# The sequence stage of a gated spectral/ReGLU kernel written as one bilinear form of 26 block products

## The chip, the core and the metric

The kernel runs on one core of a Trainium2 chip. The metric is the device time of one execution in microseconds, a median of runs. All data are float32 in HBM; a product of two float32 matrices is made of three fp32r matmuls (below).

## The reference

x has 2048 rows (positions) of 512 features, F is 1792. What is computed:

```
g = sigmoid((x * gate_w).sum(-1))
a = x @ dft_hid_re.T ; b = x @ dft_hid_im.T          # feature transform, 2048 x 512
y = dft_seq_re @ a - dft_seq_im @ b                  # sequence transform, 2048 x 2048 each
B = (relu(x @ W_gate) * (x @ W_up)) @ W_down         # ReGLU
out = g * y + (1 - g) * B
```

The change concerns the second line of the transforms, y. In the kernel dft_seq_re is called cr and dft_seq_im ci; both lie in HBM in tiles of 128 x 2 x 512 (512 KB).

## The kernel before

**One queue per engine.** Nothing loops on the chip. Python code records operations with a key, the number of matmuls after which the operation is thought to stand (op, pe), and class Plan then orders them: `due` gives each a latest time, `order` simulates the engines with fixed costs and picks what goes next on each, `run` emits the instructions in that order (all from one line, so every instruction of the profile has the line L126). On the chip each engine carries out its own queue in order; only semaphores between engines and DMAs hold it up. A key holds nothing up: a DMA that depends on nothing is issued as soon as its queue comes to it. Loads go through SP's queue (`load`), stores and accumulating DMAs (destination += source) through POOL's (`store`, `accumulate`). There are 8 semaphores for the DMAs of each of the two queues, so that a ninth waits for the first of eight.

**Split products.** A float32 operand is split in hi = its fp32r rounding (ACT, one CAST) and lo = raw - hi (DVE, one TENSOR_TENSOR); a product takes PARTS = (lo,hi), (hi,lo), (hi,hi), three matmuls. Names ending in h and l are those halves (ch, cl the two halves of a tile of Cr or Ci, wah and wal those of weights).

**SBUF** is cut into 51 units of 4 KB a partition, which the planner hands out (`buf`). PSUM is 8 banks, used as four pairs x, m, y, t (`Pair`).

**The stages, in PE's order.** A warm-up of 18 bf16 matmuls; then the two start blocks of the gate and up products (`Block`, seven products in place of eight for each 2 x 2 grid of blocks, order ORDER_S), whose tiles x11, x21, x12, x22 of x and wr of the weights are the first 12 DMAs on SP (x22 is the twelfth; DVE adds it into xs, the right side of the sixth of seven products, and wb0l is the lo part of a sum of weights of the first block, which stands behind that xs in DVE's queue); the further gate and up blocks (`Joined`, `JointX`, `JointW`), h stored to hd; the gates g (`gate`, gd); the feature transform (`Spectral`, `SpectralBlock`), whose result goes to ad in HBM; the down product (`Down(0)`, `Down(1)`, which put z, already multiplied by 1 - g, into out); then the sequence stage.

**The sequence stage before** is the last 1296 matmuls, some 291 us. It is a set of Strassen-like products with the right sides from Cr or Ci and the left sides from ad: `Joint((0,))` and `Joint((1,))` (the rows with x = 3, one for Cr and one for Ci), `Opening` twice for Cr, `Shorter` twice for Ci, and `Joint((0, 1), last=True)`. Their right sides are raw tiles or sums of tiles. `Round` and `Sequence` load raw tiles (r) and form the sums on DVE, the last of each with an accumulating DMA straight into SBUF; the Joints read theirs from td in HBM, where `joint_sums` (a copy from HBM to HBM, then an accumulation onto it) and `own_sums` (on DVE, from loaded tiles) have put them, with keys from 180 on. A product's result is taken out of PSUM at its turn, multiplied by the gate (gg) and accumulated into out. `Joint.evac` has the last rows of the kernel: the last product is made in two halves of 256 columns, each multiplied by the gate, added to what out held (jv) and stored.

Of the kernel before, what the change touches and what calls it, by code (L numbers as in the profile page):

```python
# [9 lines left out]
F32R = mybir.dt.float32r  # L10
# [19 lines left out]
FIRST = (1, 5)  # L30

# [247 lines left out]
def kernel(ctx: ExitStack, tc, xP, xG, wgu, wd, cr, ci, wri, gw, out):  # L279
# [73 lines left out]
    def combine(o, a, b, sign):  # L353
        (plan.vector.tensor_add if sign > 0 else plan.vector.tensor_sub)(o, a, b)
# [367 lines left out]
    class SpectralBlock:  # L722
# [47 lines left out]
        def out(self, f, key):  # L770
            (a11, a21), (a12, a22) = ([self.o[f"{f + 1}{j}"][:, k] for k in range(2)] for j in (1, 2))

            def keep(n, t, k=2):
                o = ad[f, n:n + k, self.q, :, 2 * self.ih:2 * self.ih + 2].rearrange("x p t n -> p x t n")
                store(o, t if k == 2 else t.unsqueeze(1))

            op(key, keep, 0, a11, 1)
            op(key, keep, 1, self.o[f"{f + 1}2"].all)
            if f == 0:
                return op(key, keep, 3, a21, 1)  # L780
            u, v = (buf(f"as{n}", (2, 2, HD)) for n in range(2))
            op(key, lambda: combine(u[:, 0], a21, a22, -1))
            op(key, lambda: combine(u[:, 1], a21, a11, -1))
            op(key + 4, lambda: combine(v[:, 0], a11, u[:, 0], -1))
            op(key + 4, lambda: combine(v[:, 1], a12, v[:, 0], -1))
            op(key + 6, keep, 3, u.all)
            op(key + 10, keep, 5, v.all)
# [35 lines left out]

    class Spectrum:


        FORM = {1: 0, 2: 1, 4: 2, 5: 3, 7: 4, 6: 5, 3: 6}

        def __init__(self):
            self.t = {}  # L830

        def get(self, m, n, key, step=8):
            raw = buf(f"l{m}", [4, HD])
            hi, lo = self.t[m, n] = [buf(f"l{x}{m}", [4, HD], F32R) for x in "hl"]
            op(key - 60, lambda: load(raw.all, ad[1, self.FORM[m], n]))
            op(key, lambda: E().scalar.copy(hi.all, raw.all))
            op(key + step, lambda: E().vector.tensor_sub(lo.all, raw.all, f32(hi.all)))

        def late(self, key):
            for m, k in ((1, 0), (5, 48), (6, 60), (7, 120), (4, 192)):  # L840
                for n in range(2):
                    self.get(m, n, key + k - 88 + 12 * n)

    SUM = {5: 40, 6: 40, 7: 44}
# [106 lines left out]
    class Sequence(Round):  # L951
        HI, LO, ONE, keep = 31, 24, 1, staticmethod(accumulate)
        FRESH = ()

        def __init__(self, left, m, p):
            self.m, self.p = m, p
            self.g = gate_row(0, (2 * p, 2 * p + 1), plan.now + 10)
            super().__init__(left, (2, 2, 2, 2))

        def parts(self):  # L960
            return [(x, jj) for x, js in ((1, 4), (5, 4), (6, 4), (3, 2), (7, 4), (3, 4), (4, 4))
                    for jj in (range(js) if (x, js) != (3, 4) else (2, 3))]

        def source(self, b, jj):
            return (cr, ci)[self.m][2 * self.p + int(b[1]) - 1, int(b[0]) - 1, jj]

        def rights(self):
            for jj in range(4):
                r = {b: buf(f"r{b}") for b in BLOCKS if b != "21"}
                for b, key in self.loads(jj):  # L970
                    op(key - 90, lambda r=r, b=b, jj=jj: load(r[b].all, self.source(b, jj)))
                for x, o, i, key in self.sums(jj):
                    if x == 4:
                        op(key, lambda r=r, o=o, jj=jj: accumulate(r[o].all, self.source("21", jj)))
                    else:
                        op(key, lambda r=r, o=o, i=i: combine(r[o].all, r[o].all, r[i].all, 1))
                for x, b in self.TILES:
                    self.split(x, jj, r[b])

        TILES = (1, "11"), (5, "11"), (6, "11"), (3, "22"), (7, "12"), (4, "11")  # L980

        def loads(self, jj):
            at = self.at
            return ("11", at[1, jj]), ("12", at[5, jj]), ("22", at[6, jj] - 10)

        def sums(self, jj):
            at = self.at
            return ((5, "11", "12", at[5, jj] - 40), (7, "12", "22", at[7, jj] - 44), (6, "11", "22", at[6, jj] - 40),
                    (4, "11", "21", at[6, jj] + 4))

    class Opening(Sequence):


        FRESH = (7, 1)
        TILES = (7, "22"), (1, "11"), (6, "22"), (5, "12"), (4, "22")

        def parts(self):
            return [(x, jj) for x, js in ((1, (0, 1)), (7, range(4)), (1, (2,)), (6, range(4)), (1, (3,)), (5, range(4)), (4, range(4)))
                    for jj in js]

        def loads(self, jj):
# [8 lines left out]
        def evac(self, x, key):  # L1010
# [9 lines left out]
            elif x == 4:  # L1020
                self.end(key)
# [421 lines left out]
```

## Time and profile before

| | |
|---|---|
| median of 3 runs | 779.41 us (779.22 to 779.71) |
| profiled execution, span | 777.9 us |
| matmuls | 3414, of them 18 for the warm-up |
| DVE, ACT, POOL instructions | 736, 499, 178 |
| HBM read, written | 155.45 MB, 74.73 MB |
| granted TensorE clock | full speed in all 40 slices |

The page gives the busy time of each engine and its share of the span; the chain is the work that ended last, followed back from the last instruction. A row of the timeline has start, length, engine, line, operation, out<-in, count, and in brackets the idle time of that engine before it and what ended it. The row of a stretch (windows) has, after its two ends and its length, the busy time of PE, PEld, DVE, ACT and POOL, then the granted clock, the DMA engines' mean busy share and GB/s. Rows of DMA issues end with the size and the time from issue to landing. q1 is SP's queue, q0 POOL's.

### The profile page before, as it was taken

To read this page: it belongs to the slowest core of one execution; us is meant where nothing else is said; L and a number is where in the kernel's file an instruction comes from. 1 tells how busy PE (TensorE), PEld (TensorE's weight loads), DVE (VectorE), ACT (ScalarE), POOL (GpSimd) and SP (SyncE) were. 2 spreads that over 40 slices of the span, in tenths; PEclk is the share of its full clock that TensorE was granted. 3 is DMA by queue.
4 is the path that set the end of the run, shared out by engine and by line. 5 is a ranking of instruction groups with operands and counts; after the bars stand their busy time and mean duration, and the time that the engine had idled before them with its cause. 6 is when DMAs were issued, how large, how long until landed. Compare 5 with 4: busy or idle time off the path is not lost.

```text
span 777.9 us, 9558 instructions
## 1 busy us (share of the span) xinstructions
PE 772.3 (99%) x3414; PEld 638.3 (82%) x3414; DVE 665.5 (86%) x736; ACT 425.9 (55%) x499; POOL 121.5 (16%) x178
## 2 busy tenths in 40 slices
PE   9999999999999999999999999999999999999997
PEld 7888888888888888888888888888888888888886
DVE  6999766766778685999996999998699899699898
ACT  6666444434455443566653667547644755345791
POOL 0021333332222332211000000030002011001000
PEclk9999999999999999999999999999999999999999
DMA  9246497999897999775369789989989997999982
GB/s 324 82 150 163 162 267 227 314 300 251 229 322 281 337 408 405 276 279 187 94 208 380 267 262 389 373 172 266 310 294 206 356 306 167 284 250 305 388 278 55
DMA packets 60255, 205.65 MB, mean 264 GB/s; under 512 B 7152, under 2 KB 7664, under 8 KB 60208
## 3 DMA queue, kind: packets, MB, share of 16 engines
q1 hardware_dynamic: 37264, 122.72, 43.5%
q0 software_dynamic: 22944, 82.32, 39.2%
q8 instruction: 27, 0.44, 0.2%
q14 instruction: 20, 0.16, 0.1%
HBM read 155.45 MB, written 74.73 MB: 296 GB/s over the span
## 4 chain that ended last, share of the span: by engine, by line
PE 98%; DMA 1%; SPq 0%; ACT 0%; DVE 0%; issue 0%; DVEq 0%
PE ps L126 98%; DMA x<-xP 1%; SPq L126 0%; DVE jo L126 0%; ACT xh L126 0%; ACT wah L126 0%; DVEq L126 0%
## 5 line engine op out<-in xcount | busy, mean ns | idle before, releaser
L126 PE MATMUL ps<-ch,ll 128*128 128x512 f32 x516 | 200.7, 389 | 0.0
L126 PE MATMUL ps<-cl,lh 128*128 128x512 f32 x516 | 200.7, 389 | 0.0
L126 PE MATMUL ps<-ch,lh 128*128 128x512 f32 x516 | 200.7, 389 | 0.0
L126 ACT CAST ch<-r 128x1024 fp32r<-128x1024 f32 x80 | 82.1, 1054 | 74.1 <-DVE r L126 64.6
L126 PEld LDWEIGHTS ps<-ch,ll 128*128 128x128 f32 x516 | 96.9, 188 | 20.1
L126 PEld LDWEIGHTS ps<-cl,lh 128*128 128x128 f32 x516 | 96.9, 188 | 20.1
L126 PEld LDWEIGHTS ps<-ch,lh 128*128 128x128 f32 x516 | 96.9, 188 | 20.0
L126 DVE TENSOR_TENSOR cl<-r,ch 128x1024 fp32r<-128x1024 f32 x80 | 95.6, 1221 | 7.7 <-ACT ch L126 6.1
L126 ACT CAST ch<-hr 128x1024 fp32r<-128x1024 f32 (+1 forms) x56 | 51.8, 945 | 43.5 <-DVE hr L126 21.2
L126 DVE TENSOR_TENSOR jcl<-jc,jch 128x1024 fp32r<-128x1024 f32 x56 | 65.6, 1222 | 7.8 <-issue 3.9
L126 ACT COPY s<-ps 128x1024 f32<-128x1024 f32 (+1 forms) x52 | 46.0, 884 | 47.6 <-PE ps L126 46.3
L126 ACT CAST jch<-jc 128x1024 fp32r<-128x1024 f32 x56 | 56.2, 1052 | 16.1 <-PE ps L126 14.0
L126 DVE TENSOR_TENSOR cl<-hr,ch 128x1024 fp32r<-128x1024 f32 (+1 forms) x56 | 60.1, 1087 | 5.1 <-ACT lh L126 2.7
L126 ACT ACTIVATE ps<-ps 128x512 f32<-128x512 f32 (+1 forms) x42 | 33.0, 785 | 55.0 <-PE ps L126 52.6
L126 POOL DMA_DIRECT2D out<-z x20 | 14.6, 729 | 297.3 <-DVE z L126 290.0
L126 DVE TENSOR_TENSOR r<-r,r 128x1024 f32<-128x1024 f32 x48 | 57.6, 1220 | 0.2
L126 DVE TENSOR_TENSOR u<-ps,s 128x1024 f32<-128x1024 f32 x28 | 34.1, 1221 | 13.4 <-PE ps L126 8.8
L126 POOL DMA_DIRECT2D hd<-h x35 | 23.0, 662 | 136.9 <-DVE h L126 125.6
L126 PE MATMUL ps<-xh,wb0l 128*128 128x512 f32 x112 | 43.8, 391 | 0.0
L126 PE MATMUL ps<-xh,wb0h 128*128 128x512 f32 x112 | 43.6, 389 | 0.0
L126 PE MATMUL ps<-xl,wb0h 128*128 128x512 f32 x112 | 43.6, 389 | 0.0
L126 PE MATMUL ps<-xh,wb1l 128*128 128x512 f32 x112 | 43.6, 389 | 0.0
(161 smaller groups left out, 1536.1 us busy)
## 6 DMA issues: line engine op xcount, KB each, us to landing
hr<-hd SPq DMA_DIRECT2D x33, 512.0 KB, 5.1
jc<-td SPq DMA_DIRECT2D x32, 512.0 KB, 8.1
td<-ci POOLq DMA_DIRECT2D x24, 512.0 KB, 10.1
r<-cr SPq DMA_DIRECT2D x24, 512.0 KB, 9.5
r<-ci SPq DMA_DIRECT2D x24, 512.0 KB, 8.5
out<-z POOLq DMA_DIRECT2D x20, 512.0 KB, 7.2
l<-ad SPq DMA_DIRECT2D x18, 512.0 KB, 8.7
wr<-wgu SPq DMA_DIRECT2D x16, 512.0 KB, 8.3
```

The costliest lines, as they stand in the source:

```text
L126: getattr(getattr(nc, self.engine), self.name)(*map(ap, self.a), **{k: ap(x) for k, x in self.k.items()})
```

## The change

y is now written as one bilinear form. Cr and Ci are taken together as a 4 x 4 grid of blocks (`block`), the feature transform as a 4 x 2 grid, and 26 products of a sum of the first with a sum of the second are added, with signs, to the 4 x 2 grid of y. TURN is the order of the products, SIDE names for each product the sum that is its right side (r), its left side (l) and the place that it is added to (o), SUMS how each sum is made of two others (sign last). Each product has four parts of 12 matmuls of 512 columns (two row tiles i, two k, three PARTS): cr and ci, two halves each.

`form_stored` puts nine of these sums, four parts each, into td by a copy from HBM to HBM and an accumulation onto it (three values from key 80 on, five from 400, one before Down(0)), `form_rights` two more by loads, DVE and a store, `form_lefts` four left sums into ad. The other sums are made in the stage: on DVE (`combine`) or, for the values in DRAWN and LDRAWN, by an accumulating DMA into the tile that is held in SBUF. `walk` decides what is held, loaded and dropped with 6 tiles (r) and 4 (l) for a part; LEAD says by how many matmuls ahead of the product's key each is done (in front of hi and lo). `Joins` holds the sums of results in PSUM pairs or, as js, in SBUF; where the next product needs the pair at once, the copy or addition is cut in two halves (`each`). The old Sequence, Opening, Shorter, Joint, Spectrum, joint_sums, own_sums and the left sides la and lb are gone, and the feature transform no longer forms sums (as) on DVE.

```diff
--- before.py
+++ after.py
+TURN = (14, 7, 10, 20, 21, 23, 13, 5, 2, 19, 6, 17, 24, 25, 11, 16, 22, 8, 4, 3, 1, 0, 18, 15, 9, 12)
+SUMS = {
+    "r": ((2, 6, -1), (6, 10, 1), (13, 15, -1), (12, 13, 1), (0, 1, 1), (9, 11, -1), (8, 17, 1), (3, 16, -1),
...
+SIDE = {
+    "r": ((26, -1), (7, 1), (29, 1), (31, -1), (32, -1), (33, 1), (22, 1), (34, -1), (25, -1), (35, 1), (16, -1),
...
+FORMED = (16, 17, 18, 19, 20, 21, 28, 30, 36, 37, 38)
+DRAWN = {34: 21, 40: 19, 42: 17, 33: 15, 29: 28, 43: 20, 25: 20, 31: 30, 26: 21}
+FLIP_T, FLIP_K = (1, -1, -1, 1), (1, 1, 1, -1)
+LFORMED = (8, 9, 11, 15)
+LDRAWN = {21: 11, 25: 8}
+ROOM = {'r': 6, 'l': 4}
+LEAD = {'r': {'load': 40, 'sum': 48, 'sums': 6, 'draws': 40, 'hi': 40, 'lo': 32}, 'l': {'load': 40, 'sum': 70, 'sums': 8, 'draws': 40, 'hi': 45, 'lo': 38}}
+RAMP = 60
...
-    ad = hbm("ad", 2, 7, 2, P, 4, HD)
+    ad = hbm("ad", 2, 8 + len(SUMS["l"]), P, 4, HD)
-    td = hbm("td", 2, 2, 4, 2, P, 2, N)
+    td = hbm("td", len(FORMED), 2, 2, P, 2, N)
...
-        (plan.vector.tensor_add if sign > 0 else plan.vector.tensor_sub)(o, a, b)
+        if sign:
+            (plan.vector.tensor_add if sign > 0 else plan.vector.tensor_sub)(o, a, b)
+        else:
+            plan.vector.scalar_tensor_tensor(o, a, -1.0, b, op0=OP.mult, op1=OP.subtract)
...
         def out(self, f, key):
...
+            for j in range(2):
+                n = 2 * (2 * self.q + j)
+                o = ad[f, n:n + 2, :, 2 * self.ih:2 * self.ih + 2].rearrange("x p t n -> p x t n")
+                op(key, lambda o=o, j=j: store(o, self.o[f"{f + 1}{j + 1}"].all))
...
+    def form_rights(values, first, last):
+        formed("r", 16, trails("r", 16, values), range(4), first, last, right_of, "rt", (2, N))
+    def form_stored(values, first, gap):
+        for n, (v, part) in enumerate((v, part) for v in values for part in range(4)):
+            a, b, _ = SUMS["r"][v - 16]
+            for i, (f, x) in enumerate(((store, a), (accumulate, b))):
+                op(first + gap * (2 * n + i), lambda f=f, x=x, v=v, part=part: f(right_of(part, v), right_of(part, x), max_dma_last_dim=8 * N))
+    def form_lefts(values, first, last):
+        formed("l", 8, trails("l", 8, values), (0, 2), first, last, left_of, "lt", (4, HD))
...
+    class Sequence:
...
+        def at(self, turn, part=0):
+            return self.base + 48 * turn + 12 * part
+        def ready(self, turn, part):
+            key = self.at(turn, part)
+            return key - max(0, RAMP - (key - self.base) / 2)
...
+            when, turn = [0] * len(plans), None
+            for n in reversed(range(len(plans))):
+                if plans[n][0] != turn:
+                    turn, key = plans[n][0], lead["sum"]
+                kind = plans[n][1]
+                if kind in ("sum", "draw"):
+                    key += lead[kind + "s"]
+                when[n] = key + lead["load"] if kind == "load" else key
...
+                    if kind == "load":
+                        b = held[v] = buf(side, shape)
+                        op(at, lambda b=b, v=v, part=part: load(b.all, source(part, v)))
+                        last[id(b)] = at
...
+                    elif kind == "draw":
+                        o = held[v] = held.pop(how[0])
+                        at = max(at, last.get(id(o), -999) + 1)
+                        op(at, lambda o=o, y=how[1], part=part: accumulate(o.all, source(part, y)))
+                        last[id(o)] = at
...
+            joins = Joins(self)
+            for turn, product in enumerate(TURN):
+                (rv, rg), (lv, lg), (ov, og) = (SIDE[x][product] for x in "rlo")
+                ps, fresh, sign = joins.begin(turn, ov, SIGNS["r"][rv] * rg * SIGNS["l"][lv] * lg * og)
+                for part in range(4):
+                    c = self.split("c", (2, N), *r[turn, part], False)
+                    if part % 2 == 0:
+                        w = self.split("w", (4, HD), *l[turn, part], sign < 0)
+                    pe(12, self.product, ps, w, c, part, fresh)
+                joins.end(turn, ov)
+        def product(self, ps, w, c, part, fresh):
+            hh = part % 2
+            for i in range(2):
+                for k in range(2):
                     for n, (a, b) in enumerate(PARTS):
-                        mm(ps, l[a][:, 2 * hh + i], c[b][:, i, cols], start=x in FIRST and begin and i == n == 0,
-                           stop=x not in (1, 5, 6, 7) and end and i == 1 and n == 2)
+                        mm(ps[i], w[a][:, 2 * hh + k, i * P:(i + 1) * P], c[b][:, k],
+                           start=fresh and part == k == n == 0, stop=part == 3 and k == 1 and n == 2)
...
+        def each(self, split, f, *a):
+            key = self.at(self.turn + 1) - 1
+            if not split:
+                self.early = 0
+                return op(key, lambda: f(*(x.all for x in a)))
+            for n in range(2):
+                op(key - self.early * (1 - n), lambda n=n: f(*(x[n] if isinstance(x, Pair) else x[:, n] for x in a)))
...
+        def tail(self, x, sign, t, d, g, key):
+            o, v = buf("z"), buf("v")
+            op(key - 100, lambda: load(v.all, od[t, :, 2 * d:2 * d + 2]))
+            for i in range(2):
+                op(key, lambda i=i: E().vector.scalar_tensor_tensor(o[:, i], x[i], float(sign), g.all, op0=OP.mult, op1=OP.mult))
+                op(key, lambda i=i: combine(o[:, i], o[:, i], v[:, i], 1))
+                op(key, lambda i=i: load(od[t, :, 2 * d + i], o[:, i]))
...
-    for n in range(4):
-        joint_sums(n // 2, 2, n % 2, 180 + 110 * n)
-    for n in range(2):
-        own_sums(0, 3, n, 1200 + 100 * n)
-    for n in range(2):
-        joint_sums(1, 3, n, 620 + 110 * n)
+    form_stored([16, 18, 19], 80, 11)
+    form_stored([20, 21, 28, 30, 36], 400, 18)
+    form_rights([17, 37], 1100, 1500)
...
-    la = Left(lambda b, n: ad[0, {"11": 0, "12": 1, "22": 2, "21": 3}[b], n])
-    lb = Spectrum()
...
+    form_stored([38], plan.now - 20, 20)
     Down(lw, 0)
...
+    form_lefts([8, 9, 11, 15], plan.now - 250, plan.now + 50)
     Down(lw, 1)
-    Joint((0,), "xm", 3, [la.side(3, n) for n in range(2)])
-    opened = Opening(la, 0, 0).carry()
-    lb.late(plan.now + 324)
-    Joint((1,), "xm", 3)
-    Opening(la, 0, 1)
-    Shorter(lb, 1, 1)
-    opened.resume(plan.now - 10)
-    Shorter(lb, 1, 0)
-    Joint((0, 1), "xm", last=True, lead=(80, 30))
+    Sequence().run()
```

**What moves.** POOL's queue from its first DMA on, names with their buffer numbers and what a row waits for (DVE is DVE's semaphore, DMASW0 to 7 those of POOL's own DMAs); hd<-h are the stores of the first blocks' h, td sums of Cr or Ci tiles. Before:

```order
L126 DMA hd_68<-h0_214 128x512 [waits DVE_49] x2
L126 DMA hd_68<-h0_242 128x512
L126 DMA hd_68<-h0_242 128x512 [waits DVE_49]
L126 DMA hd_68<-h1_428 128x2x512 [waits DVE_49]
L126 DMA hd_68<-h1_449 128x2x512 [waits DVE_49]
L126 DMA td_70<-cr 128x1024
L126 DMA td_70<-cr 128x1024 [waits DMASW6_49]
```

After:

```order
L262 DMA td_70<-cr 128x1024 x2
L262 DMA td_70<-cr 128x1024 [waits DMASW0_49]
L262 DMA td_70<-ci 128x1024
L262 DMA td_70<-cr 128x1024 [waits DMASW1_49]
L262 DMA td_70<-ci 128x1024
L262 DMA td_70<-ci 128x1024 [waits DMASW3_49]
L262 DMA td_70<-cr 128x1024
L262 DMA td_70<-ci 128x1024 [waits DMASW5_49]
L262 DMA hd_68<-h0_214 128x512 [waits DVE_49]
L262 DMA hd_68<-h0_214 128x512 [waits DMASW2_49,DVE_49]
```

Nine transfers into td, the first two without a wait, now stand ahead of the first store of h; before they began behind six of these stores.

DVE's last rows; cl, jcl are lo parts, wl that of the left side, ps is PSUM, gg the gate, jv and v what out held. Before:

```order
L126 TENSOR_TENSOR jcl_6208<-jc_5982,jch_6180 128x1024
L126 TENSOR_TENSOR jo1_6192<-ps_75,js_6052 128x512
L126 TENSOR_TENSOR jo1_6192<-jo1_6192,gg_5990 128x512
L126 TENSOR_TENSOR jo1_6192<-jo1_6192,jv1_6012 128x512
L126 TENSOR_TENSOR jo0_6231<-ps_75,gg_5990 128x512
L126 TENSOR_TENSOR jo0_6231<-jo0_6231,jv0_5870 128x512
L126 TENSOR_TENSOR jo0_6231<-ps_75,gg_5990 128x256
L126 TENSOR_TENSOR jo0_6231<-jo0_6231,jv0_5870 128x256
L126 TENSOR_TENSOR jo0_6231<-ps_75,gg_5990 128x256
L126 TENSOR_TENSOR jo0_6231<-jo0_6231,jv0_5870 128x256
```

After:

```order
L262 TENSOR_TENSOR wl_6006<-l_5776,wh_5997 128x1024
L262 TENSOR_TENSOR cl_6013<-r_5897,ch_5932 128x1024
L262 TENSOR_TENSOR cl_6020<-r_5919,ch_5948 128x1024
L262 TENSOR_TENSOR z_6027<-ps_75,gg_5869 128x1024
L262 SCALAR_TENSOR_TENSOR z_6048<-ps_75,gg_5953 128x512
L262 TENSOR_TENSOR z_6048<-z_6048,v_5923 128x512
L262 SCALAR_TENSOR_TENSOR z_6048<-ps_75,gg_5953 128x512
L262 TENSOR_TENSOR z_6048<-z_6048,v_5923 128x512
```

The last product is no longer cut into halves of 256 columns: its four rows have 512 each, and ahead of them stands the multiplication of the product before it.

POOL's queue in the first third of the sequence stage (r, r22 and l are tiles in SBUF that the DMA adds to; z and jo go to out). Before:

```order
L126 DMA out<-z21_3937 128x1024 [waits DMASW4_49,DVE_49]
L126 DMA out<-jo1_4047 128x1024 [waits DMASW5_49,DMASW1_49,DVE_49]
L126 DMA out<-jo0_4054 128x1024 [waits DMASW6_49,DVE_49]
L126 DMA out<-z12_4188 128x1024 [waits DMASW7_49,DMASW6_49,DVE_49]
L126 DMA r22_3953<-cr 128x1024 [waits DMAHW3_49,DMASW0_49,Activation_49]
L126 DMA r22_3980<-cr 128x1024 [waits DMAHW0_49,Activation_49]
L126 DMA r22_4005<-cr 128x1024 [waits DMAHW2_49,DMAHW6_49,DMASW2_49,DVE_49]
L126 DMA r22_4033<-cr 128x1024 [waits DMAHW0_49,DMAHW5_49,DMASW3_49,DVE_49]
L126 DMA out<-z21_4490 128x1024 [waits DMASW4_49,DVE_49]
```

After:

```order
L262 DMA r_3613<-td_70 128x1024 [waits DMAHW2_49,DMAHW4_49,DMASW5_49,DVE_49]
L262 DMA r_3654<-td_70 128x1024 [waits DMASW6_49,DVE_49]
L262 DMA r_3690<-td_70 128x1024 [waits DMAHW2_49,DMASW7_49,DVE_49]
L262 DMA r_3723<-td_70 128x1024 [waits DMASW0_49,DVE_49]
L262 DMA r_3912<-td_70 128x1024 [waits DMASW1_49,DVE_49,PE_49]
L262 DMA r_3936<-td_70 128x1024 [waits DMASW2_49,DMAHW3_49,DVE_49,PE_49]
L262 DMA l_3599<-ad_69 128x1024 [waits DMAHW4_49,DMASW3_49,Activation_49]
L262 DMA r_3958<-td_70 128x1024 [waits DMASW4_49,DVE_49]
L262 DMA r_3983<-td_70 128x1024 [waits DMASW5_49,DVE_49,PE_49]
L262 DMA l_3698<-ad_69 128x1024 [waits DMASW6_49,Activation_49]
```

Accumulations into r come in groups of four with the stores of z between, now from td, and into l from ad; before there was one such group for each round.

More of the change, by code (lines that the diff above doesn't have):

```diff
@@ new lines, in trails @@
+def trails(side, blocks, values):
+    left, found = {v: SUMS[side][v - blocks][:2] for v in values}, []
+    while left:
+        ends = [x for e in left.values() for x in e]
+        x = min(ends, key=lambda x: (1 - ends.count(x) % 2, x))
+        trail = [(x, None)]
+        while True:
+            v = next((v for v, e in left.items() if x in e), None)
+            if v is None:
+                break
+            a, b = left.pop(v)
+            x = b if x == a else a
+            trail.append((x, v))
+        found.append(trail)
+    return found
```

512 lines of the change are left out of this document (252 added, 260 removed), and 7 rows, old and new, of the table SUMS.

## The prediction

> **What bounds the kernel now.** I read the page first, then the chain, then what ended PE's waits.
>
> The page's busy times, DMA queues and chain, and three pieces of the chain in order of time (start, length, what):
>
> ```profile
> PE 772.3 (99%) x3414; PEld 638.3 (82%) x3414; DVE 665.5 (86%) x736; ACT 425.9 (55%) x499; POOL 121.5 (16%) x178
> q1 hardware_dynamic: 37264, 122.72, 43.5%
> q0 software_dynamic: 22944, 82.32, 39.2%
> PE 98%; DMA 1%; SPq 0%; ACT 0%; DVE 0%; issue 0%; DVEq 0%
> 11.23 761.70 PE ps L126 x3366
> 774.28 0.42 DVE jo L126
> ```
>
> PE runs without a gap from 11.23 us to 772.93 us. So the time is start + matmuls + tail. One matmul of 512 columns costs 761.70 / 3366 = 0.2263 us (the few of 256 columns pull this down a little; between two starts in the middle of the trace lie 0.227 us). DVE is 86% busy and the 16 DMA engines 43.5 + 39.2 = 83%: neither sets the time, but neither is far from it, and whatever holds PE up once is paid in full, because nothing later on PE is idle that could take it in.
>
> The span of the profiled execution is 777.9 us, the median of the timed runs 779.41 us: 1.5 us lie around the span, and I add them at the end.
>
> **Matmuls taken out.** Counted in the sequence stage: before 1296 matmuls, 24 of them of 256 columns; after 26 products x 4 parts x 12 = 1248, all of 512. Outside the stage nothing changes on PE. That is 36 of 512 and 24 of 256 columns fewer, worth 36 + 12 = 48 of 512: 48 x 0.2265 = **-10.9 us**. This holds where PE stays fed.
>
> **DVE and ACT in the stage.** DVE has 671 rows for 712, and its load falls. The tightest row of before:
>
> ```profile
> 480.00:520.00 40.00, 40.00 (x178) 33.13 (x177) 39.74 (x38) 24.40 (x27) 4.87 (x6) 1.00 0.91 304
> L126 DVE TENSOR_TENSOR cl<-r,ch 128x1024 fp32r<-128x1024 f32 x80 | 95.6, 1221 | 7.7 <-ACT ch L126 6.1
> ```
>
> At 480 to 520 us DVE was busy 39.74 of 40 us and PE still did not wait. After, one turn is 48 matmuls = 10.9 us, and the 1.13 us between starts of such rows (1221 ns, pipelined) lets 9.6 of them pass. The densest place is the end of turn 23: four js rows, one cl, three multiplications by the gate and then the lo part of the next weights, 9 x 1.13 = 10.2 us. That fits by 0.7 us. Some turns begin on a PSUM pair that ACT or DVE has just copied or added in two halves; six matmuls (1.36 us) cover a half of 0.6 to 0.7 us. I count these at **0**; the cover gone would cost 0.5 us each, for six places at most 3 us.
>
> **The tail.** Last rows of before on DVE, and the stores behind them:
>
> ```profile
> 773.03 0.42 DVE L126 TENSOR_TENSOR jo<-ps,gg 128x256 f32<-128x256 f32 x1 [0.38 <-PE ps L126]
> 771.96 0.69 DVE L126 TENSOR_TENSOR jo<-jo,jv 128x512 f32<-128x512 f32 x1
> out<-jo SPq DMA_DIRECT2D x2, 256.0 KB, 3.1
> out<-jo SPq DMA_DIRECT2D x2, 128.0 KB, 1.9
> ```
>
> Before, from PE's end to the last DVE row's end 1.8 us pass (772.93 to 774.70), then a store of 128 KB (1.9 us to landing). After, two of the four last rows, of 512 columns each, remain behind the last matmuls, 0.69 + 0.69 = 1.4 us, and a store of 256 KB, 3.1 us. So -0.4 + 1.2 = **+0.8 us**, between 0 (if the store lands as the small one) and 1.5.
>
> **The POOL queue at the start.** This is the term that decides. POOL carries out its queue in order and waits only for semaphores. Rows of POOL, SP, ACT, DVE and PE in before (start, length; in brackets the idle time before and what ended it):
>
> ```profile
> 17.84 0.71 POOL L126 DMA_DIRECT2D hd<-h  x1 [17.39 <-DVE h L126]
> 51.71 0.56 POOL L126 DMA_DIRECT2D td<-cr  x1
> 4.71 0.88 PE L126 MATMUL ps<-xh,wah 128*128 128x512 f32 x2
> 6.41 0.74 SPq L126 DMA_DIRECT2D x<-xP  x1
> 15.99 1.05 ACT L126 CAST xh<-x 128x1024 fp32r<-128x1024 f32 x1 [0.53 <-DMA x<-xP]
> 17.44 1.22 DVE L126 TENSOR_TENSOR xs<-x,xs 128x1024 f32<-128x1024 f32 x1
> 18.57 0.69 DVE L126 TENSOR_TENSOR wb0l<-ws,wb0h 128x512 fp32r<-128x512 f32 x1
> 19.57 0.40 PE L126 MATMUL ps<-xh,wb0l 128*128 128x512 f32 x1
> 10.00:22.00 12.00, 11.46 (x51) 9.11 (x50) 11.75 (x16) 9.38 (x14) 0.71 (x1) 1.00 1.03 411
> 22.00:50.00 28.00, 28.00 (x124) 22.79 (x123) 27.86 (x36) 18.50 (x24) 2.35 (x4) 1.00 0.18 67
> ```
>
> Before, the first DMA on POOL waits for DVE's h until 17.84 us, and the first sum of Cr blocks (td) goes out at 51.71 us. In the DMA-heavy start (share 1.03 from 10 to 22 us) SP's queue is therefore alone. After, nine td transfers, 5 copies and 4 accumulations, stand ahead of the first hd<-h, and the first two wait for nothing: they go out at about 0.7 us. The planner's key of 80 matmuls stands in no semaphore. They share the engines with the loads that PE waits for.
>
> The software queue's share from 2 to 22 us, and from issue to landing of POOL's first transfer and of the first td row, each alone in its window:
>
> ```profile
> q0 software_dynamic: 16, 0.07, 0.8%
> hd<-h POOLq DMA_DIRECT2D x1, 256.0 KB, 6.0
> td<-cr POOLq DMA_DIRECT2D x1, 512.0 KB, 5.7
> ```
>
> Price of one, from a window in which both queues were loaded (600 to 609 us; packets, MB, share), POOL's packets there being accumulations almost alone:
>
> ```profile
> q0 software_dynamic: 337, 1.22, 68.4%
> q1 hardware_dynamic: 334, 1.23, 36.4%
> ```
>
> A packet of the hardware queue took 0.364 x 9 x 16 / 334 = 0.157 us of one engine, an accumulating one 0.684 x 9 x 16 / 337 = 0.292 us. At 82.32 MB / 22944 packets, 512 KB are 146 packets: 1.43 us of all 16 engines for a copy, 2.66 us for an accumulation. All nine: 5 x 1.43 + 4 x 2.66 = 17.8 us. And the queues took turns packet by packet (337 to 334), so SP's loads do not go first.
>
> [...]
>
> What the loads can stand: x22, issued at 6.41 us, landed at 15.99 us. DVE needs it for xs at 17.44 us, and behind xs stands wb0l, 1.13 + 0.69 us, which PE takes at 19.57 us. So xs may start at 17.75, and x22 land 1.8 us late, at no cost; what is beyond that, D, stops PE, and DVE with it. x22 is the last load of the first two blocks that is close to its use.
>
> - Lower end: only the first two copies get in ahead, on the first loads, which have no such slack (PE waits for them at 4.71 us): D = 2 x 1.43 = 2.9 us.
> - Upper end: all nine before x22: 17.8 - 1.8 = 16.0 us.
> - Between: the accumulations wait for the copy they add to. A td transfer took 5.7 us to land in a quiet stretch, more in a full one, so the chain copy, accumulation, copy passes POOL's six first rows (4 copies, 2 accumulations = 11.0 us) by about 12 us, and the last three rows (6.8 us) start at 17 to 22 us, when x22 would be still outstanding. Six wholly and a quarter of the other three: 11.0 + 1.7 - 1.8 = **+10.9 us**. I take this.
>
> From 22 to 50 us the DMA share was 0.18, so the loads behind x22 find room for the rest.
>
> **DMA in the sequence stage.** After, accumulations rise from 57 to 83 and POOL's share of the engines with them; SP's loads fall from 142 to 116 of 512 KB in the stage.
>
> ```profile
> 520.00:580.00 60.00, 60.00 (x267) 49.69 (x266) 51.78 (x50) 36.99 (x40) 2.54 (x3) 1.00 0.94 294
> 580.00:640.00 60.00, 60.00 (x266) 49.73 (x265) 57.25 (x51) 34.42 (x36) 8.62 (x10) 1.00 0.98 281
> r<-cr POOLq DMA_DIRECT2D x4, 512.0 KB, 14.9
> ```
>
> The engines were already 94 to 98% busy there. By the prices above, an estimate for the whole span: SP's queue 338 us less 26 x 1.43, POOL's 305 us plus 26 x 2.66 and some copies, 680 us together of 768, 89%. An accumulation into r took 14.9 us to land (560 to 600 us). The code puts it 88 matmuls (19.9 us) ahead of PE's use and 48 (10.9 us) ahead of its hi part. So the slowest of before would be 4 us late for its hi part, with 5 us left for hi and lo (1.05 + 1.22 us): not late for PE. I count **0**; lower end 0, since PE has no wait there to lose; upper end 8 us, if each of the eleven groups of accumulations (nine into r, two into l) held PE up by 0.7 us.
>
> **Sum.** 777.9 - 10.9 + 0.8 + 10.9 + 0 = 778.7 us of span, + 1.5 = **780.2 us**: the matmuls saved are given back at the start.
>
> **Rivals.**
> - *The start is cheap.* D is 2.9 to 6 us: the copies from HBM to HBM get few turns while SP's queue is full. For it: hd<-h, issued at 17.84 us into a full queue, is a store of 256 KB that took 6.0 us to land. Against it: two td rows need nothing and are ahead of the first load. Time: 777.9 - 10.9 + 0.8 + 2.9 to 6 + 1.5 = 772.2 to 775.3 us. [...]
> - *Accumulations land late* (the other side). The start costs what I say, and in the sequence stage accumulations into r and l land too late. ACT stands at the hi part, PSUM copies and the next hi parts queue behind it, then lo on DVE, and PE waits for those. By the lead of 19.9 us less hi, lo and a row or two ahead of each in their queues, it decides from a landing of about 15.5 us on. Price 3 to 8 us: 783.2 to 788.2 us. For it: DMA at 89%, 14.9 us already seen. Against it: PE waited nowhere in such stretches before.
> - *The matmuls do not vanish as counted*, or the start costs nothing at all: D = 0 gives 769.3 us. The rows of POOL are against this.
>
> **Chances.** Forecast 0.50, cheap start 0.28, late accumulations 0.20, nothing lost 0.02. A measurement of this kernel tells apart about 0.2%, 1.56 us: faster is below 777.85 us, slower above 780.97. Within the forecast D spreads from 6 to 16 us: below 8.6 is faster (0.08), to 11.7 the same (0.24), above slower (0.18). With the rivals: faster 0.38, same 0.24, slower 0.38. The forecast's own range, D from 8.5 to 14, is 777.8 to 783.3 us. The whole range must take in the cheap start and most of the late accumulations: 771.5 to 787.
>
> **What would show it.** POOL's timeline: td rows from about 0.7 us on, the first hd<-h later than 17.84 us. The DMA queues between 2 and 22 us: a software share of 30 to 60% where before it had 0.8% (right), or under 15% (cheap start). PE's waits: a sum of some 11 us ended by xh, xl or wb0l rows, all before 35 us, x22 landing at about 28 us. Behind that PE should run on to its end with no wait over 0.5 us; waits ended by ACT ch or DVE cl between 470 and 760 us show late accumulations. From PE's end to the span's end: 5.8 us for 5.0. Wrong altogether would be a PE that waits for DVE at the starts of turns, or a gap at turn 24.

## The result, and the profile after

The changed kernel took 788.45 us (median of 4 runs, 785.71 to 790.74), the kernel before 779.47 us beside it (779.22 to 779.71): ratio 1.0114, 95% interval 1.0092 to 1.0135. It is slower, and it lies above the range of 771.5 to 787 us. Its runs also lie 5 us apart, those of the kernel before 0.5 us. The profiled execution took 788.1 us, with a span of 786.3 us.

The page of the changed kernel, busy times, DMA queues and chain:

```profile
PE 769.3 (98%) x3354; PEld 631.9 (80%) x3354; DVE 643.1 (82%) x694; ACT 402.8 (51%) x472; POOL 147.7 (19%) x212
q0 software_dynamic: 28608, 103.56, 50.4%
q1 hardware_dynamic: 32800, 109.08, 37.4%
PE 73%; DMA 13%; issue 6%; DVE 4%; POOL 2%; ACT 1%; SPq 0%; POOLq 0%; DVEq 0%; ACTq 0%
```

The 60 records of matmuls fewer, the lighter DVE and ACT and POOL's larger share are as counted. But PE is only 73% of the chain: DMAs and DVE have come into it. What ended PE's waits:

```profile
PE ps L262 <- ACT wah L262: 3.8, 2, 3.6
PE ps L262 <- ACT s L262: 2.8, 1, 2.8
PE ps L262 <- DVE wb0l L262: 2.2, 2, 1.9
PE ps L262 <- DVE h L262: 1.0, 1, 1.0
PE ps L262 <- PEq L1530: 0.8, 1, 0.8
PE ps L262 <- DVE cl L262: 0.7, 2, 0.4
```

And before:

```profile
PE ps L126 <- PEq L1436: 0.8, 1, 0.8
PE ps L126 <- ACT wah L126: 0.5, 1, 0.5
```

These are 11.3 us, more than the 1.3 of before by 10.0, and that is not all of it. A window's row has the number of matmuls that PE started in it; three windows of the changed kernel, then the same three of the kernel before (where a count falls short, PE stood still or ran slowly):

```profile
0.00:40.00 40.00, 32.18 (x123) 24.19 (x124) 24.23 (x36) 20.70 (x31) 6.90 (x14) 0.91 0.94 314
260.00:300.00 40.00, 37.22 (x152) 30.22 (x151) 18.00 (x33) 15.82 (x22) 11.36 (x16) 0.91 1.03 365
400.00:440.00 40.00, 39.32 (x173) 31.89 (x172) 39.72 (x39) 19.40 (x22) 4.25 (x8) 1.00 0.96 356
```

```profile
0.00:40.00 40.00, 38.68 (x167) 30.37 (x168) 33.55 (x48) 25.94 (x36) 0.92 (x5) 1.00 0.54 197
260.00:300.00 40.00, 40.00 (x178) 33.15 (x177) 24.53 (x33) 17.23 (x22) 11.85 (x19) 1.00 1.02 399
400.00:440.00 40.00, 40.00 (x178) 33.14 (x177) 32.51 (x31) 20.05 (x22) 1.62 (x3) 1.00 0.92 330
```

Up to 40 us 44 matmuls are missing (x 0.2265 = 10.0 us), from 260 to 300 us 26 (5.9 us), from 400 to 440 us 5 (1.1 us). Elsewhere up to 440 us the counts agree within one in each of eight windows of 20 to 60 us. Behind 440 us, the whole sequence stage, PE's waits list no wait at all.

**The start.** Rows of POOL's timeline (the other five of the nine td transfers lie between them), then the row of ACT that waits for x22, then the queues' shares from 2 to 22 us:

```profile
1.26 1.24 POOL L262 DMA_DIRECT2D td<-cr  x2 [0.82 <-POOLq L1530]
8.21 0.83 POOL L262 DMA_DIRECT2D td<-cr  x1 [5.70 <-DMA td<-cr]
19.90 0.83 POOL L262 DMA_DIRECT2D td<-ci  x1 [8.75 <-DMA td<-ci]
26.79 0.86 POOL L262 DMA_DIRECT2D hd<-h  x1
```

```profile
25.75 1.05 ACT L262 CAST xh<-x 128x1024 fp32r<-128x1024 f32 x1 [4.96 <-DMA x<-xP]
```

```profile
q1 hardware_dynamic: 1637, 3.92, 53.5%
q0 software_dynamic: 686, 2.55, 44.2%
```

The td rows go out from 1.26 us, not at the 18 us of their key, and the first hd<-h at 26.79 us in place of 17.84. They have 44.2% of the engines' time, and x22 lands at 25.75 us in place of 15.99.

**The wait at 272 us** is new. The chain around it, in order of time:

```profile
251.23 10.97 DMA hd<-h
262.22 10.67 DMA x<-xP
273.86 1.01 ACT s L262
274.92 136.38 PE ps L262 x588
```

A store of h that POOL issued at 250.5 us landed at 262.2 us. SP's queue waited for it, for a unit of SBUF to come free, and issued the load of x only then; the load took 10.67 us, the hi part of x stood in ACT's queue ahead of the copy s out of PSUM, and PE waited for s. It paid twice, for behind the wait it ran at half its clock, 0.50 from 276 to 280 us (the number behind POOL's is the granted clock):

```profile
272.00:276.00 4.00, 1.22 (x4) 0.89 (x4) 0.58 (x1) 1.96 (x2) 0.92 (x1) 0.77 1.02 419
276.00:280.00 4.00, 4.00 (x11) 3.13 (x10) 3.18 (x9) 0.68 (x2) 0.00 (x0) 0.50 1.03 422
280.00:284.00 4.00, 4.00 (x16) 3.22 (x16) 2.82 (x3) 1.46 (x3) 2.13 (x3) 0.87 1.05 376
```

A wait of 2.78 us thus cost 5.9.

### The profile page after: what moved, and what is told of

It is laid out like the page before. It is cut to its first block, busy times and chain, and to the rows that moved or that the text cites. A ratio compares the mean times of both kernels' runs of the same rounds, so it can differ in the third digit from the quotient of the medians.

```text
span 786.3 us, 9315 instructions
## 1 busy us (share of the span) xinstructions
PE 769.3 (98%) x3354; PEld 631.9 (80%) x3354; DVE 643.1 (82%) x694; ACT 402.8 (51%) x472; POOL 147.7 (19%) x212
## 3 DMA queue, kind: packets, MB, share of 16 engines
q0 software_dynamic: 28608, 103.56, 50.4%
q1 hardware_dynamic: 32800, 109.08, 37.4%
## 4 chain that ended last, share of the span: by engine, by line
PE 73%; DMA 13%; issue 6%; DVE 4%; POOL 2%; ACT 1%; SPq 0%; POOLq 0%; DVEq 0%; ACTq 0%
PE ps L262 73%; DMA td<-cr 5%; DMA x<-xP 3%; DMA td<-ci 2%; DMA hd<-h 1%; DMA r<-td 1%; DVE cl L262 1%; DMA wr<-wgu 1%; POOL td L262 1%; DVE z L262 1%; POOL hd L262 0%; DVE hr L262 0%; POOL r L262 0%; DVE h L262 0%; ACT ch L262 0%
## 5 line engine op out<-in xcount | busy, mean ns | idle before, releaser
L262 PE MATMUL ps<-ch,wl 128*128 128x512 f32 x416 | 162.3, 390 | 0.1
L262 PE MATMUL ps<-ch,wh 128*128 128x512 f32 x416 | 161.9, 389 | 0.0
L262 PE MATMUL ps<-cl,wh 128*128 128x512 f32 x416 | 161.8, 389 | 0.0
L262 PEld LDWEIGHTS ps<-ch,wl 128*128 128x128 f32 x416 | 78.1, 188 | 17.4 <-ACT js L262 0.7
L262 PEld LDWEIGHTS ps<-ch,wh 128*128 128x128 f32 x416 | 78.1, 188 | 16.4
L262 PEld LDWEIGHTS ps<-cl,wh 128*128 128x128 f32 x416 | 78.1, 188 | 16.1
L262 PE MATMUL ps<-cl,lh 128*128 128x512 f32 x196 | 76.5, 390 | 0.7 <-DVE cl L262 0.7
L262 PE MATMUL ps<-ch,ll 128*128 128x512 f32 x196 | 76.3, 389 | 0.0
L262 PE MATMUL ps<-ch,lh 128*128 128x512 f32 x196 | 76.3, 389 | 0.0
L262 ACT CAST ch<-hr 128x1024 fp32r<-128x1024 f32 (+1 forms) x56 | 51.6, 944 | 33.0 <-DVE hr L262 16.5
L262 DVE TENSOR_TENSOR wl<-l,wh 128x1024 fp32r<-128x1024 f32 x40 | 48.6, 1218 | 0.1
```

The costliest lines, as they stand in the source:

```text
L262: getattr(getattr(nc, self.engine), self.name)(*map(ap, self.a), **{k: ap(x) for k, x in self.k.items()})
```

## The experiments

Ratios are against the kernel before in the same batch (779.5 to 779.7 us).

### The start's part put into the kernel before: early_in_before

```diff
-        joint_sums(n // 2, 2, n % 2, 180 + 110 * n)
+        joint_sums(n // 2, 2, n % 2, 60 + 20 * n)
```

> The kernel before with one edit: the first four calls of joint_sums have their keys at 60 + 20n in place of 180 + 110n, so that nine td transfers (5 copies, 4 accumulations) stand ahead of the first hd<-h, as in the changed kernel; nothing else of the change. Theory S (the start is lost to these nine transfers): x22 lands at 25 to 28 us, PE waits before 35 us sum to 6 to 9 us, and the time is 779.5 + 8 to 11 = 787.5 to 790.5 us. Rival (the start of the changed kernel is lost to something else of the change): x22 lands near 16 us, 779 to 780 us.

Measured: 794.33 us, ratio 1.0191 (1.0176 to 1.0206), +14.6 us. x22's hi part starts at 31.74 us, and up to 40 us PE has 103 matmuls for 167, 14.5 us fewer: all of the loss. The rival falls; but the loss is larger than expected from the same nine rows. Here three copies wait for nothing, in the changed kernel two.

### The start's part taken out of the changed kernel: late

```diff
-    form_stored([16, 18, 19], 80, 11)
+    form_stored([16, 18, 19], 200, 8)
```

> The changed kernel with its first form_stored at keys from 200 with a gap of 8 in place of 80 and 11, so that the six first hd<-h stand ahead of all td transfers. Theory S: x22 lands near 16 us, the waits before 35 us shrink to 0.5 us, the time falls by 9 to 10 us to 777 to 780 us, and the wait near 272 us stays (2 to 3 us, with matmuls at half the clock behind it). Rival (the DMA engines are short as a whole, and what is moved costs the same elsewhere): the time stays at 785 to 789 us, with new waits behind 50 us.

Measured: 775.14 us (774.26 to 775.71), ratio 0.9936 (0.992 to 0.9953). PE has 168 matmuls up to 40 us, as before the change. 13.3 us came back, more than the start's 10: the wait near 272 us shrank too, to 0.29 and 0.83 us. So the two were not parted by this run, and Theory S alone does not give it. The rival, that the transfers cost the same anywhere, falls.

### The order of copies and accumulations: grouped, late_grouped, group2

```diff
-        for n, (v, part) in enumerate((v, part) for v in values for part in range(4)):
+        for n, (v, i, part) in enumerate((v, i, part) for v in values for i in range(2) for part in range(4)):
...
-            for i, (f, x) in enumerate(((store, a), (accumulate, b))):
+            for f, x in (((store, a), (accumulate, b))[i],):
```

> The changed kernel with form_stored putting out the four copies of a sum first and then its four accumulations, in place of copy, accumulation, copy, accumulation; keys and number of transfers as they were. Theory Q (the wait near 272 us comes from POOL's queue: stores of h stand behind td accumulations that wait for the copy just ahead of them, the SBUF units of h come free late, and the load of x is issued late): POOL's idle time ended by td landings falls from 160 to under 90 us, the load of x goes out before 250 us, no wait of PE near 272 us, and the time falls by 4 to 6 us to 782 to 785 us; the start stays as slow. Rival (the DMA engines are full from 260 to 300 us and the load is late for that): the wait stays at 2 to 4 us and the time at 786 to 790 us.

> Both edits of late and grouped. If S and Q hold, both losses go: 777.9 - 10.9 + 0.8 + about 1.5 of small waits + 1.7 around the span = 771 to 774 us, faster than before. If only S: 776 to 779 us. If neither: 785 us and more.

Measured: grouped 788.26 us (ratio 1.0111, 1.0096 to 1.0126), late_grouped 779.5 us (0.9997, 0.9988 to 1.0006). Grouped has its 178 matmuls from 260 to 300 us (POOL's waits for td landings fell from 160 to 31 us), but by now four copies without a wait lead the queue, and up to 40 us it has 100 matmuls, 15.2 us lost. Late_grouped has the start and 260 to 300 us whole, and a new wait: 4.3 us at 124.6 us, for lo parts of weights (wal). Their two loads, issued at 98.9 and 102.1 us, landed 10 us later; but DVE made wal only at 123.29 us, behind eleven rows of u, h and jws, where in the kernel before it did so at 112.14 us and ahead of the first of those u. Plan orders every queue anew from the keys, so an edit of td's keys can move rows of DVE as well; how much of the 4.3 us is the loads and how much this order was not parted. Neither total was met, though the wait that each edit was made to remove did go.

The second group alone, the start untouched (in group2 and the kernels named after it form_stored has a parameter for it):

```diff
-    form_stored([20, 21, 28, 30, 36], 400, 18)
+    form_stored([20, 21, 28, 30, 36], 400, 18, 4)
```

> The changed kernel, its first nine td transfers untouched; only the second form_stored (keys from 400) puts out four copies of a sum and then its four accumulations. This parts the wait near 272 us from the start. Theory Q: the start loses the same 10 us as in the changed kernel (125 matmuls recorded up to 40 us, 168 before), from 260 to 300 us PE has 176 to 179 matmuls in place of 153, and the time is 788.4 - 5 to 6 = 782 to 784 us. Rival (that wait follows from the delayed start, or from full DMA engines): it stays, 786 to 790 us.

Measured: 781.4 us (780.47 to 782.56), ratio 1.0023 (1.0013 to 1.0032), 7.0 us less than the changed kernel. Up to 40 us 127 matmuls, the start as slow as in the changed kernel; from 260 to 300 us 178. What POOL's td rows waited for from 90 to 300 us, in the changed kernel and then in group2, and the load of x in group2's SP queue:

```profile
POOL td L262 <- DMA td<-cr: 60.0, 10, 11.4
POOL td L262 <- DMA td<-ci: 54.9, 11, 10.2
```

```profile
POOL td L262 <- DMA td<-cr: 3.8, 1, 3.8
POOL td L262 <- DMA td<-ci: 2.4, 1, 2.4
```

```profile
252.56 0.70 SPq L262 DMA_DIRECT2D x<-xP  x1
```

With the same transfers in the same stretch and nearly the same late start, 115 us of waiting in POOL's queue become 6, the load of x goes out at 252.56 in place of 262.22 us, and the wait is gone. The load itself lands no faster (11.4 us for 10.67), and the DMA engines are as full as before (1.03 from 260 to 300 us), so that fullness alone was not the cause. Of the 7.0 us the profiles put 5.9 on this wait and 0.9 on the start (127 matmuls for 123). So the order of td's transfers in POOL's queue is what decides, as theory Q has it. Its way to the load of x is less simple. POOL's rows in the changed kernel, then in group2:

```profile
230.56 0.85 POOL L262 DMA_DIRECT2D td<-cr  x1 [11.37 <-DMA td<-cr]
233.01 0.81 POOL L262 DMA_DIRECT2D td<-ci  x1 [1.60 <-DMA td<-ci]
233.55 2.14 POOL L262 DMA_DIRECT2D hd<-h  x3
250.47 1.34 POOL L262 DMA_DIRECT2D hd<-h  x2 [0.94 <-DVE h L262]
```

```profile
226.72 1.86 POOL L262 DMA_DIRECT2D hd<-h  x3 [11.49 <-DVE h L262]
247.27 1.33 POOL L262 DMA_DIRECT2D hd<-h  x2 [15.33 <-DVE h L262]
```

Three stores of h do stand behind the waits for td and go out 6.8 us later. The two stores that SP's queue waits for do not: ahead of them POOL is idle until DVE has made h. They go out 3.2 us later than in group2 and land in 11 us in place of 5. In the 3.6 us before them three td transfers had gone out, while in group2 the last had gone out 16.5 us before. So the longer landing, and not the holding up, is the larger part of the 9.7 us; that those three transfers cause it is likely, but was not tested alone.

### Both together, and smaller edits

Late_group2 is late with the second group's line of group2.

> The first form_stored behind the stores of h (keys from 200, gap 8, copy and accumulation in turn), the second with four copies and then four accumulations. If the start (about 10 us) and the wait near 272 us (about 6 us in the changed kernel) are two losses with two causes, they add up: 788.4 - 10 - 6 = 772 to 773 us, with 168 matmuls up to 40 us, 178 from 260 to 300, and only the small waits at 124 us (wb0l) and 413 to 420 us (cl) left. If the grouping only moved the jam, as a rival, 776 us and more.

Measured: 777.95 us (776.12 to 780.45), ratio 0.9982 (0.9972 to 0.9992); 5 us more than the sum of the two gains would give, and 2.8 us more than late without the grouping. The start (169) and 260 to 300 us (178) are whole; a wait of 3.31 us for wb0l stands at 126 us. The rival has it: a part of the jam had moved.

Spread, against late:

```diff
-    form_stored([16, 18, 19], 200, 8)
-    form_stored([20, 21, 28, 30, 36], 400, 18)
+    form_stored([16, 18, 19], 190, 12)
+    form_stored([20, 21, 28, 30, 36], 480, 16)
```

> Against late (775.1 us): first form_stored at keys from 190 with a gap of 12, second from 480 with a gap of 16; same transfers, less dense from 45 to 115 us. Theory: the remaining wait at 124 us (1.2 us, a late load of wr behind td transfers) goes, and the time is 773 to 775 us. Rival: POOL issues as soon as it can, so the keys change little, 775 to 776 us.

Measured: 777.58 us (775.47 to 785.0), ratio 0.9981 (0.9962 to 1.0001). The wait at 123 us shrinks to 0.17 us as expected, but the ungrouped transfers now go on longer (the last of them is issued at 277.83 us, in late at 268.65), and PE has new waits of 0.40 and 2.00 us at 401 to 404 us, for ch and cl. That the one causes the other was not shown. Neither expected total was met.

Gap9_group2_tail, against late_group2_tail (below):

```diff
-    form_stored([16, 18, 19], 200, 8)
+    form_stored([16, 18, 19], 190, 9)
```

> The same as late_group2_tail with the first form_stored at keys from 190 and a gap of 9. The wait at 124 us (1.2 us, weights that come late behind td transfers) should shrink: 0 to 1 us less than late_group2_tail. If POOL's keys hold nothing up, the rival, no difference within 0.5 us.

Measured: 774.93 us (774.47 to 775.06), ratio 0.9937 (0.9925 to 0.9949), 3.6 us less than late_group2_tail, more than was looked for: the rival falls. The wait for wb0l shrank from 3.31 to 0.75 us, with another of 1.13 us ahead of it, at 119.8 us. But the keys did not thin the stretch out: from 60 to 135 us the software queue had this share, in late_group2_tail and then here:

```profile
q0 software_dynamic: 5371, 19.45, 96.7%
q0 software_dynamic: 5422, 19.62, 97.9%
```

Spread_group2, against late_group2:

```diff
-    form_stored([16, 18, 19], 200, 8)
-    form_stored([20, 21, 28, 30, 36], 400, 18, 4)
+    form_stored([16, 18, 19], 190, 12)
+    form_stored([20, 21, 28, 30, 36], 480, 15, 4)
```

> The first form_stored at keys from 190 with a gap of 12, the second grouped by four at keys from 480 with a gap of 15. From 60 to 135 us POOL's queue filled the DMA engines (97.9% of their time in gap9_group2_tail) and the weights for 120 us came late; this takes transfers out of that stretch. Theory: no wait over 0.5 us before 300 us, 772 to 774 us. Rival: the transfers now run into the stretch from 240 us on, and loads there come late: 775 to 778 us.

Measured: **772.67 us** (772.4 to 773.02), ratio **0.9909** (0.9894 to 0.9924), faster than both kernels. All that PE waited for:

```profile
PE ps L262 <- PEq L1530: 0.8, 1, 0.8
PE ps L262 <- DVE cl L262: 0.7, 2, 0.4
PE ps L262 <- ACT wah L262: 0.5, 2, 0.3
PE ps L262 <- DVE wb0l L262: 0.3, 2, 0.2
```

It makes the same products by the same transfers as the changed kernel (28608 and 32800 packets in the two queues, in both). Only the keys and the order of td's transfers differ, with what Plan makes of them in the other queues, and that is worth 15.8 us.

Late_lefts, against late:

```diff
-    form_lefts([8, 9, 11, 15], plan.now - 250, plan.now + 50)
+    form_lefts([8, 9, 11, 15], plan.now - 150, plan.now + 130)
```

> Against late: form_lefts from now - 150 to now + 130 in place of now - 250 to now + 50, because DVE is full up to 420 us and has room from 430 to 460. Theory: the two waits ended by cl at 413 and 416 us (0.7 us, with 1.4 us of matmuls lost) go: 773.5 to 774.5 us. Rival: the 14 loads of lt fall into a stretch in which the DMA engines are full, and r or l land later: 775 to 778 us.

Measured: 781.46 us, ratio 1.0026 (1.0012 to 1.0039). This is the rival's mechanism, at more than its price of 775 to 778 us: between 469 and 488 us PE waits five times, 0.2 to 1.7 us, on hi and lo parts that come late. Of the waits for cl near 415 us one of 0.46 us is left; in all other kernels made from the changed one such waits, between 400 and 430 us, sum to 0.7 to 2.0 us.

### The price of one transfer at the start: two_early

```diff
+                op(first + gap * (2 * n + i) if first > 200 or n > 1 or i else 80, lambda f=f, x=x, v=v, part=part: f(right_of(part, v), right_of(part, x), max_dma_last_dim=8 * N))
```

> As late, but with only the first two copies into td (no accumulation) ahead of the first hd<-h, so that they go out at about 1 us. This measures my price of a transfer at the start. By 1.43 us of all engines each, the loads that PE waits for are 2.9 us late: 775.1 + 2.9 = 778 us, with 13 matmuls fewer than late up to 40 us. If the price is that of a transfer that holds the queue of loads up for longer, 4 to 8 us: 779 to 783 us. If the two copies alone hide in the slack before PE's first real matmul: 775 us.

Measured: 779.12 us (776.54 to 782.55). 145 matmuls up to 40 us for 168 of late: 5.2 us for two copies of which the prediction's estimate makes 2 x 1.43 = 2.9. PE waited 3.99 us for weights at 10.76 us, and its clock was 0.96 in the mean of the window. For the start the middle answer, 4 to 8 us, has the size, but not its reason: PE's waits for wah are 3.3 us longer than in late (4.3 for 1.0), near the 2.9, and most of the rest is slow matmuls behind them (0.43 us from start to start between 12.56 and 15.12 us, 0.23 from 15.67 us on). (Its profiled run has another 2.1 us of wait near 268 us, so the total says less.)

| kernel | td rows ahead of hd<-h | of them without a wait | matmuls to 40 us | lost |
|---|---|---|---|---|
| late | 0 | 0 | 168 | 0 |
| two_early | 2 | 2 | 145 | 5.2 us |
| changed kernel | 9 | 2 | 123 | 10.0 us |
| early_in_before | 9 | 3 | 103 | 14.5 us |
| grouped | 9 | 4 | 100 | 15.2 us |

The losses do not follow the number ahead of hd<-h. They follow how many of these transfers had been issued by 16 us, when x22 has landed in late (its cast starts at 15.88 us): 0, 2, 6, 8 and 9, in the order of the table. The packets of POOL's queue from 2 to 22 us rise with them: 18, 288, 686, 845 and 951. In these five kernels what counts is how many get to the engines before x22 has landed.

### The tail: late_tail, late_group2_tail

```diff
-            for i in range(2):
-                op(key, lambda i=i: E().vector.scalar_tensor_tensor(o[:, i], x[i], float(sign), g.all, op0=OP.mult, op1=OP.mult))
...
+            half = slice(0, N // 2), slice(N // 2, N)
+            for i, c in ((0, slice(0, N)), (1, half[0]), (1, half[1])):
+                op(key, lambda i=i, c=c: E().vector.scalar_tensor_tensor(o[:, i, c], ps8[:, x.n + i, c], float(sign), g[:, c], op0=OP.mult, op1=OP.mult))
...
```

> Against late: the last row tile of the last product is multiplied, added and stored in two column halves of 256, the first row tile as it was. By the term of the tail, the last store is of 128 KB (1.9 us to landing for 2.7) and DVE's rows behind PE 1.4 us as before: 0.5 to 1.0 us less, 774.1 to 774.7 us. If the store's size does not matter at the end: 775.1 us.

> The same with the last row tile of the last product multiplied, added and stored in two column halves of 256. Beside late_group2 alone this shows the term of the tail without the wait near 265 us, which comes and goes from run to run in late: 0.5 to 1.0 us less than late_group2. If the store's size does not matter at the end: no difference.

Measured: 776.04 us (773.25 to 778.15) against late's 775.14, and 778.54 us (777.57 to 779.83) against late_group2's 777.95. No gain, in scatter larger than what was looked for. The profiles show it better: from the start of the last matmul to the end of the span pass 5.8 us in late_group2 and 5.7 us in gap9_group2_tail. The size of the last store is not what sets the end: of the last stores those of 256 KB landed in 2.8 us in late_group2, those of 128 KB in 2.6 in gap9_group2_tail. What does (0.52 MB in POOL's queue, where the accumulation of z was issued at 765.63 us, still move from 767 us on in late_group2) was not tried.

## Why the prediction was wrong

By its own steps, against the profiled execution (span 786.3 us, forecast 778.7):

- **Matmuls, -10.9 us: right.** PE runs its last pieces at 0.227 us a matmul, and spread_group2, with hardly a wait, has a span of 771.0 us: 777.9 - 10.9, and some 4 us of small losses.
- **DVE and ACT in the stage, 0: right.** No wait behind 440 us is listed; the turns that begin on a half did not show, nor the end of turn 23. The 1.1 us lost between 400 and 440 us, by waits for cl at 425 and 429 us, lie ahead of the stage and had no term. DVE was full there (39.72 of 40 us), but late has the same waits with DVE at 34.41, so their cause is open.
- **The tail, +0.8: mis-sized.** The last rows of PE, before and after:

```profile
773.36 0.28 PE L126 MATMUL ps<-jch,jwh 128*128 128x256 f32 x1
```

```profile
780.30 0.39 PE L262 MATMUL ps<-ch,wh 128*128 128x512 f32 x1
```

  From there to the end 4.5 and 6.0 us: +1.5, the bound that was given. The wrong part is a reading: 772.93 us is where the chain passes from PE to DVE, not PE's end. Before, PE's last matmul runs to 773.64 us, so that 1.1 us and not 1.8 pass to the end of DVE's last row; after, it is 1.4. So the part of DVE is about +0.4, where the prediction has -0.4.
- **The start, +10.9: right in mechanism and size, 10.0.** But that the size fits is luck: x22 landed at 25.75 us for some 28 forecast, and the product that takes wb0l behind xs started at 28.19 us in place of 19.57, 8.6 us late. Matmuls at a lower clock behind that wait (0.61 from 28 to 30 us, 0.54 from 30 to 32, 0.91 in the mean up to 40 us), which no term had, make up the rest. The largest single wait, 3.60 us at 10.21 us, was for the first weights (wah), which the prediction names only at its lower end.
- **DMA in the sequence stage, 0: right.** But the 15.5 us at which a landing was to decide is not borne out. Accumulations into r took 9.9 us in the median there, two issued between 560 and 590 us took 20.2 in the median, the longest 21.0, and PE still waited for none of them; ACT did, at most 5.0 us.
- **The step that failed** is the one sentence with which the start was closed: from 22 to 50 us "the loads behind x22 find room for the rest". It looked 28 us ahead. The other td transfers of form_stored, up to 275 us, had no term at all. In POOL's queue, in order, each accumulation waits for the copy just ahead of it, and the stores of h behind go out late or land late among the td transfers; a unit of SBUF comes free 9.7 us later than in group2, SP's load into it goes out late, and at 272 us PE waits 2.8 us and loses 5.9 with the clock. Group2, with nothing edited but the order of these transfers, is 7.0 us shorter and has no such wait.

The sum of what was measured: 777.9 - 10.9 + 10.0 + 5.9 + 1.1 + 1.5 = 785.5 us, of 786.3.

Of the rivals, none happened. The cheap start is excluded by early_in_before, where the nine transfers alone cost 14.5 us, and by the 44.2% of the engines' time that POOL's transfers had from 2 to 22 us in the changed kernel; late accumulations by the stage's empty list of waits.

## What to carry to other kernels

A key in a planner is a wish. If no semaphore carries it, a queue in order makes it true only by what stands ahead, and a transfer that waits for nothing goes to the front of the program, where the loads are that everything waits for (the first td<-cr at 1.26 us, where its key stood for 18). When transfers are added to a queue, follow what stands behind each of their waits to the buffers that it frees, through the whole program, not only where the transfers are used; and put dependent pairs apart (four copies, then four accumulations), so that the wait is over when the queue comes to it (in group2 115 us of such waits became 6). That alone is not enough: it gained 7.0 us in group2 and 4.9 in spread_group2 against spread, but in late_group2 it cost 2.8 against late, and in grouped, at the start, the loss rose from 10.0 to 15.2 us. Each order of the transfers has to be followed through the program again.

## What the runs showed of the hardware

A wait of PE was often, not always, followed by some microseconds at a lower granted clock. Behind 40 us the profiles have seven waits of 2.00 to 4.34 us. Behind six of them the clock fell:

| run | wait of PE | behind it |
|---|---|---|
| changed kernel | 2.78 us, to 274.92 us | clock 0.50 from 276 to 280 us |
| two_early | 2.14 us, to 270.21 us | matmuls start 0.43 us apart from 271.61 to 274.59 us, then 0.23; clock 0.96 from 260 to 300 us |
| late_tail | 2.5 us, for s, between 260 and 300 us | clock 0.96 from 260 to 300 us |
| spread | 2.00 us, to 403.64 us | clock 0.69 from 403 to 407 us, 0.88 to 411 us |
| late_grouped | 4.34 us, to 124.56 us | clock 0.83 from 120 to 130 us |
| late_group2_tail | 3.31 us, to 126.47 us | clock 0.50 from 126 to 130 us |
| late_group2 | 3.31 us, to 126.39 us | clock 1.00 from 126 to 130 us |

The length alone does not decide: in late_lefts the clock was 0.60 from 476 to 480 us behind waits of 0.73 and 0.96 us, and 1.00 from 487 to 491 us behind one of 1.74 us.

Late_group2 and late_group2_tail both wait 3.31 us for wb0l at 126 us; the window behind it in the one, then in the other:

```profile
126.00:130.00 4.00, 3.61 (x16) 2.99 (x17) 3.97 (x7) 1.09 (x2) 1.02 (x2) 1.00 1.07 209
```

```profile
126.00:130.00 4.00, 3.53 (x8) 2.81 (x9) 3.96 (x7) 0.62 (x1) 0.95 (x2) 0.50 1.07 210
```

16 matmuls against 8, at a granted clock of 1.00 and of 0.50. Over 40 to 260 us that is 953 against 941, 2.7 us of difference from the same wait; it fits the scatter of the kernels that wait (776.1 to 780.5 us in late_group2) beside those that don't (772.4 to 773.0 in spread_group2), and the mean clock of each execution: in late_group2 0.999 in the two below 777 us, 0.993 to 0.997 in the four above 779.
